# Dummy matmuls and a split weight wait at the start of an attention and GEGLU kernel

## The chip, the cores and the metric

The kernel runs on one NeuronCore of one Trainium2 chip. Its engines are TensorE (PE, the matrix unit; PEld are its weight loads), VectorE (DVE), ScalarE (ACT), GpSimd (POOL) and SyncE (SP). They run side by side and wait for one another on semaphores. SP, ACT and POOL each have a queue on which they issue transfers; the 16 DMA engines of the core serve all of them. The metric is the device time of one execution in microseconds.

## The reference

One sequence of 2048 rows of width 448 goes through a layer norm. The normed rows feed two branches: attention with 16 query heads of width 256 over the last 512 entries of a cache with 8 key and value heads, and a feed-forward network of width 1792. The second branch gates the first.

```python
xn = _layernorm(x)                                  # x: 2048 x 448
q  = xn @ wq                                        # 16 heads x 256
p  = softmax(q @ k[-512:].T * 256**-0.5)            # 8 key heads, each for 2 query heads
s  = (p @ v[-512:]).reshape(2048, 4096) @ wo
g  = silu((gelu(xn @ w_gate) * (xn @ w_up)) @ w_down)
out = x + s * g
```

All inputs and the output are bfloat16.

## The kernel before

The rows are 16 tiles of 128 (t = 0 to 15), and four tiles are one chunk of 512 columns of the transposed activations `xnT`. The width 448 is three blocks of 128 and a rest of 64: `wgu` holds the gate and up weights of the first 384 input rows (k = 0, 1, 2), `wgur` those of the last 64 rows (k = 3, `NK`), gate's on partitions 0 to 63 and up's on 64 to 127.

**Order of the work.** It is written out by hand. Every `K.op` goes to the end of its engine's program; `Plan` finds the waits from the buffers that each operation reads and writes. Operations of PE that write after one another into the same bank do not wait, except where `after` names an operation. An engine runs its program in order, so an operation that waits holds up everything behind it on that engine.

**Stages.** First the head: layer norm of tiles 0 to 3, their transposes by PE and the first feed-forward units of chunk 0. Then the feed-forward units of all four chunks (gate, up, gelu, product), with the down projections between them, then the q projections, scores, softmax, weighted sums and the output projection, chunk by chunk. The layer norm and the transposes of the tiles from 4 on run beside the feed-forward units.

**Loads at the start** (L345 to L352). SP issues x tile 0, the first block of gate weights, x tile 2 and the last rows of gate's first block; ACT issues x tile 1, the first block of up weights, x tile 3 and the last rows of up's first block. Then SP goes on with the other tiles and weight blocks; ACT issues no more.

**The head on PE** (L520 to L552). `warm(20, 3)` issues 20 matmuls on a zeroed buffer into bank 3, whose result nothing reads. `ln_tp_pe(0, ...)` transposes tile 0 in two parts, k = 1, 2 into banks 6 and 7 and k = 0, 3 into banks 4 and 5, and ACT copies each part into `xnT` (L424 to L427). Then `gu_group(HEAD, PH, (0, 1), ((0, 0), (0, 1)))` (L529) starts the units f = 0, 1, 2 on the columns of tile 0 with bank pairs (0, 1), (2, 3) and (4, 5): three passes of part 0 (k = 2, 1), then three of part 1 (k = 0 and the last rows). Each of the six passes has four matmuls of 64 rows and 128 columns. Then come the transposes of tile 1, the second phase of the units on tile 0, the units on tile 1, and so on through tile 3.

**A pass** (`group`, L440 to L463). A unit has a gate bank and an up bank; phase 0 multiplies the upper half of the rows for one and the lower half for the other, and phase 1 the other way round. The last rows (`NK`) belong to phase 0 alone. Each pass waits for all of `reads`, which L473 makes of the unit's weight block, its last rows (`b_wlr`) and a placeholder for the whole weight region. `last_row[b]` remembers the last pass on a bank pair and its phase: a pass of another phase waits for that one on the semaphore of PE.

**DVE's order in the head** is statistics of tiles 0 and 1, scaling of tile 0 and 1, statistics of tile 2, statistics of tile 3, scaling of tile 2, scaling of tile 3. ACT computes the standard deviations and copies the transposes out of PSUM.

Of the kernel before, what the change touches and what calls it, by code (L numbers as in the profile page):

```python
# [11 lines left out]
P = 128  # L12
# [152 lines left out]
def bass_recurrent_scan__sliding_block_cached__geglu_ffn__prompt_kernel(  # L165
# [19 lines left out]
    QC = 512  # L185
# [5 lines left out]
    NK = D // P  # L191
# [6 lines left out]
    HG = 8  # L198
# [3 lines left out]
    with es:  # L202
        K = Plan(nc, es)
        base = [(nc.sbuf_base + 31) // 32 * 32]

        def place(name, shape, dt, at=None):
            size = {BF16: 2, F32: 4}[dt]
            for n in shape[1:]:
                size *= n
            size = (size + 31) // 32 * 32  # L210
            if at is None:
                at = base[0]
                base[0] += size
            assert at + size <= nc.sbuf_usable_end, (name, at + size, nc.sbuf_usable_end)
            return nc.alloc_sbuf_tensor_at(name, list(shape), dt, offset=at), at, at + size

        def sbuf_bufs(at, size, n):
            return [K.buf(at + i * size, size) for i in range(n)]
# [26 lines left out]
        b_xnT = [[K.buf(), K.buf()] for t in range(NT)]  # L245
# [7 lines left out]
        wqr, a, _ = place("wqr", [P, Hq, P], BF16)  # L253
        b_wql = [[K.buf() for i in range(3)] for g in range(NG)]
# [21 lines left out]
        b_wgu = K.buf(a, at - a)  # L276
        FBL = [0, 3, 6, 9, NF]
        b_wl = [[K.buf() for j in range(2)] for i in range(4)]
        b_wlr = [[K.buf() for j in range(2)] for i in range(3)]
# [6 lines left out]
        b_gl = sbuf_bufs(a, QC * 2, NGL)  # L286
# [18 lines left out]
        b_ps = [K.buf() for i in range(8)]  # L305
# [4 lines left out]
        def qs(h):  # L310
            return HG - 1 - h % HG


        def dma(q, o, i, reads=(), writes=()):
            K.op(q, lambda e, o=o, i=i: e.dma_start(o, i), reads, writes, dma=True)  # L315
# [4 lines left out]
        def act(o, i, func, reads, writes, scale=1.0):  # L320
            K.op("act", lambda e, o=o, i=i: e.activation(o, i, func, scale=scale), reads, writes)  # L321

        def mms(lst, reads, writes, after=()):
            def fn(e):
                ins = None
                for (o, l, r, st, sp) in lst:
                    ins = e.matmul(o, lhsT=l, rhs=r, start=st, stop=sp)  # L327
                return ins
            return K.op("pe", fn, reads, writes, after=after)


        def load_x(q, t0, n):
            dma(q, x4[:, t0:t0 + n, :], x_view[:, t0:t0 + n, :], (), b_x4[t0:t0 + n])
# [6 lines left out]
        def load_wr(q, i, j):  # L340
            w = (B_w_gate, B_w_up)[j]
            lo, hi = FBL[i] * P, (FBL[i + 1] if i < 2 else NF) * P
            dma(q, wgur[R * j:R * j + R, lo:hi], w[K3:D, lo:hi], (), (b_wlr[i][j],))
# [3 lines left out]
        load_w("sp", 0, 0)  # L347
        load_w("act", 0, 1)
        load_x("sp", 2, 1)
        load_x("act", 3, 1)  # L350
        load_wr("sp", 0, 0)
        load_wr("act", 0, 1)  # L352
        K.op("pool", lambda e: e.memset(ident[:, :], 0.0), (), (b_ident,))
        K.op("pool", lambda e: e.affine_select(
            out=ident[:, :], in_=ident[:, :], compare_op=ALU.not_equal, fill=1.0, base=0,
# [32 lines left out]
        def ln_recip(t):  # L388
            K.op("dve", lambda e: e.reciprocal(rstd[:, t:t + 1], ve[:, t:t + 1]), (b_ve[t],), (b_rstd[t],))
# [18 lines left out]
        def ln_tp_pe(t, parts):  # L408

            s = t % NXN  # L410
            for i, b in parts:
                tp = pall[b // 2].bitcast(BF16)[:, :].rearrange("p (b k c) -> p k b c", b=2, c=R)
                ks = {None: slice(0, NK + 1), 0: slice(1, 3), 1: slice(0, 4, 3)}[i]

                def fn(e, tp=tp, ks=ks):
                    ins = None
                    for k in range(NK + 1)[ks]:
                        for u in range(2):
                            r = slice(R * u, R * u + R)
                            ins = e.transpose(tp[:, k, u, :], xn[r, s, k * P:(k + 1) * P], ident[r, r])  # L420
                    return ins
                K.op("pe", fn, (b_xn[s][:1] if i == 0 else b_xn[s]) + [b_ident], b_ps[b:b + 2])
            for i, b in parts:
                tp = pall[b // 2].bitcast(BF16)[:, :].rearrange("p (b k c) -> p k b c", b=2, c=R)  # L424
                ks = {None: slice(0, NK + 1), 0: slice(1, 3), 1: slice(0, 4, 3)}[i]
                act(xnT[:, ks, t * P:(t + 1) * P].rearrange("p k (b c) -> p k b c", c=R), tp[:, ks, :, :],
                    ACT.Copy, b_ps[b:b + 2], b_xnT[t] if i is None else b_xnT[t][i:i + 1])  # L427

        def warm(n, b):
            def fn(e):  # L430
                ins = None
                for i in range(n):
                    ins = e.matmul(bank[b][:, 0:256], lhsT=gl[:, 0, 0:P], rhs=gl[:, 0, 0:256], start=True, stop=True)
                return ins
            K.op("pe", fn, (b_gl[0],), (b_ps[b],))


        last_row = {}

        def group(units, lo, hi, start, stop, phases=(0, 1)):  # L440

            for p in phases:
                ph, part = p if isinstance(p, tuple) else (p, None)
                ks = {None: [2, 1, 0, NK], 0: [2, 1], 1: [0, NK]}[part]
                for (b, w, wr, cols, reads, xts) in units:
                    lst = []  # L450
                    for k in ks:
                        if k == NK and ph == 1:
                            continue
                        for u, j in ((0, ph), (1, 1 - ph)):
                            rows = slice(R * u, R * u + R)
                            l = wr[rows] if k == NK else w(j, k)[rows]
                            lst.append((bank[b + j][:, lo:hi], l, xnT[rows, k, cols], start and ph == 0 and k == 2,
                                        stop and ph == 1 and k == 0))
                    before = [last_row[b][0]] if b in last_row and last_row[b][1] != ph else []
                    xb = [y for x in xts for y in (x if part is None else x[part:part + 1])]  # L460
                    o = mms(lst, reads + xb, b_ps[b:b + 2], before)
                    last_row[b] = (o, ph)

        def gu_group(ns, pairs, part=None, phases=(0, 1)):

            lo, hi = (0, QC) if part is None else (part[0] * P, part[1] * P)
            units = []
            for n, b in zip(ns, pairs):
                c, f = divmod(n, NF)
                wi = [j for j in range(4) if FBL[j] <= f][-1]  # L470
                fc = slice(f * P, (f + 1) * P)
                units.append((b, lambda j, k, fc=fc: wgu[:, j, k, fc], wgur[:, fc], slice(c * QC + lo, c * QC + hi),
                              b_wl[wi] + b_wlr[min(wi, 2)] + [b_wgu], b_xnT[c * 4 + lo // P:c * 4 + hi // P]))  # L473
            group(units, lo, hi, lo == 0, hi == QC, phases)

        def bk(pairs, j):
# [21 lines left out]
        def ln_first(t):  # L498
            ln_stats(t)
            ln_std_act(t)  # L500

        def ln_second(t, dup="dve"):
            ln_recip(t)
            ln_norm(t, dup)
# [9 lines left out]
        def ln_b():  # L514
            if ln_t[1] < ln_t[0]:
                ln_norm(ln_t[1])
                ln_tp_dma(ln_t[1])
                ln_t[1] += 1

        warm(20, 3)  # L520
        ln_first(0)
        ln_first(1)
        ln_second(0)
        ln_tp_pe(0, ((0, 6), (1, 4)))
        ln_second(1, "act")
        HEAD, PH = (0, 1, 2), (0, 2, 4)
        T = ((None, 6),)
        ln_first(2)
        gu_group(HEAD, PH, (0, 1), ((0, 0), (0, 1)))  # L529
        ln_tp_pe(1, T)  # L530
        ln_first(3)
# [72 lines left out]
        def q_group(c, h, pairs):  # L604

            units = [(b, lambda j, k, i=i: wq[:, k, (h + i) * Dh + j * P:(h + i) * Dh + (j + 1) * P],
                      wqr[:, h + i, :], slice(c * QC, (c + 1) * QC), b_wql[h // HG], b_xnT[c * 4:c * 4 + 4])
                     for i, b in enumerate(pairs)]
            group(units, 0, QC, True, True)
            for i, b in enumerate(pairs):  # L610
                s = qs(h + i)
                act(qT[:, s, 0, :], bank[b], ACT.Copy, (b_ps[b],), (b_qT[s][0],))
                K.op("dve", lambda v, s=s, b=b: v.tensor_copy(qT[:, s, 1, :], bank[b + 1]),  # L613
                     (b_ps[b + 1],), (b_qT[s][1],))
# [92 lines left out]
        c = NQC - 1  # L707
# [11 lines left out]
        for i in range(2):  # L719
            b = (AB[3], BB[0])[i]  # L720
            lo, hi = ((0, CUT), (CUT, D))[i]
# [57 lines left out]
```

## Time and profile before

| what | value |
|---|---|
| median of 4 runs | 558.36 us (557.53 to 559.59) |
| profiled execution | 559.59 us |
| its span, first to last instruction | 557.8 us |
| PE busy | 549.8 us, 99% of the span |
| DVE, ACT busy | 316.9 us, 274.3 us |
| granted clock of PE | 1.00 |

The span is what the trace covers; about 1.8 us of the profiled execution lie around it. All times in the prediction's rows are microseconds from the start of the span. A row of the time line gives start, duration, engine, line, operation, output and inputs, and in brackets how long the engine had been idle and what ended that. A line can be that of a helper: L327 is every matmul of `mms`, L420 the transposes, L433 the dummy matmuls, L321 ACT's copies and activations, L315 every plain DMA. In rows of DMA issues the last number is the time from issue to landing in us. A table of stretches gives for each stretch its length, the busy time and number of instructions of PE, PEld, DVE, ACT and POOL, the granted clock, the DMA engines' busy share (over 1 where packets overlap) and GB/s.

### The profile page before, as it was taken

To read this page: it belongs to the slowest core of one execution; us is meant where nothing else is said; L and a number is where in the kernel's file an instruction comes from. 1 tells how busy PE (TensorE), PEld (TensorE's weight loads), DVE (VectorE), ACT (ScalarE), POOL (GpSimd) and SP (SyncE) were. 2 spreads that over 40 slices of the span, in tenths; PEclk is the share of its full clock that TensorE was granted. 3 is DMA by queue.
4 is the path that set the end of the run, shared out by engine and by line. 5 is a ranking of instruction groups with operands and counts; after the bars stand their busy time and mean duration, and the time that the engine had idled before them with its cause. 6 is when DMAs were issued, how large, how long until landed. Compare 5 with 4: busy or idle time off the path is not lost.

```text
span 557.8 us, 9780 instructions
## 1 busy us (share of the span) xinstructions
PE 549.8 (99%) x3650; PEld 265.9 (48%) x3650; DVE 316.9 (57%) x816; ACT 274.3 (49%) x728; POOL 32.7 (6%) x64
## 2 busy tenths in 40 slices
PE   7999999999999999999999999999999999999997
PEld 5664444444544444454444445544444454444455
DVE  6683624444377686515848753286685515858722
ACT  4342323444386685504848752085785504758600
POOL 1120750000000000000000000000000000000000
PEclk9999999999999999999999999999999999999999
DMA  9560599501166284312716713166364313807701
GB/s 290 104 163 9 160 292 324 110 1 39 38 114 115 57 152 96 75 35 71 154 37 142 142 25 87 35 139 105 74 153 77 77 34 88 153 20 151 149 11 34
DMA packets 163599, 57.63 MB, mean 103 GB/s; under 512 B 151456, under 2 KB 160672, under 8 KB 163552
## 3 DMA queue, kind: packets, MB, share of 16 engines
q1 hardware_dynamic: 159488, 45.16, 38.9%
q0 software_dynamic: 3296, 11.27, 6.5%
q8 instruction: 29, 0.48, 0.4%
q10 hardware_dynamic: 768, 0.57, 0.3%
q14 instruction: 18, 0.15, 0.1%
HBM read 17.92 MB, written 1.84 MB: 35 GB/s over the span
## 4 chain that ended last, share of the span: by engine, by line
PE 98%; DMA 1%; issue 0%; SPq 0%; ACT 0%; DVE 0%
PE bank L327 98%; DMA wgur<-in_B_w_gate_dram 1%; SPq L315 0%; ACT xnT L321 0%; PE bank L420 0%; DVE tmp L666 0%; DVE ofin L669 0%
## 5 line engine op out<-in xcount | busy, mean ns | idle before, releaser
L627 ACT ACTIVATE p<-bank 128x512 f32<-128x512 f32 x256 | 149.2, 597 | 103.3 <-PE bank L327 102.0
L631 DVE TENSOR_SCALAR pn<-p,rden 128x512 bf16<-128x512 f32 x256 | 124.5, 486 | 16.9 <-DMA pT<-pn 8.0
L327 PE MATMUL bank<-kT,qT 128*128 128x512 bf16 x512 | 121.0, 379 | 0.0
L327 PE MATMUL bank<-pT,va 128*128 128x512 bf16 x512 | 120.8, 379 | 0.0
L327 PE MATMUL bank<-wo,oT 128*128 128x448 bf16 (+2 forms) x544 | 97.7, 341 | 0.0
L327 PE MATMUL bank<-xnT,wq 64*128 64x512 bf16 x768 | 94.7, 376 | 0.0
L327 PE MATMUL bank<-xnT,wgu 64*128 64x512 bf16 (+1 forms) x780 | 84.4, 347 | 3.4 <-DMA wgur<-in_B_w_gate_dram 1.4
L327 PEld LDWEIGHTS bank<-pT,va 128*128 128x128 bf16 x512 | 50.0, 98 | 60.6 <-DMA pT<-pn 0.7
L327 PEld LDWEIGHTS bank<-kT,qT 128*128 128x128 bf16 x512 | 49.5, 98 | 61.6 <-issue 3.4
L327 PEld LDWEIGHTS bank<-wo,oT 128*128 128x128 bf16 x544 | 52.0, 98 | 45.5
L613 DVE CAST qT<-bank 128x512 bf16<-128x512 f32 x64 | 42.9, 692 | 49.3 <-PE bank L327 49.3
L321 ACT ACTIVATE qT<-bank 128x512 bf16<-128x512 f32 x64 | 38.2, 597 | 61.1 <-PE bank L327 59.4
L327 PEld LDWEIGHTS bank<-xnT,wq 64*128 64x128 bf16 x768 | 36.8, 94 | 46.8 <-ACT p L627 1.7
L483 DVE TENSOR_TENSOR actT<-bank,gl 128x512 bf16<-128x512 f32 x56 | 37.8, 690 | 35.5 <-PE bank L327 26.7
L327 PEld LDWEIGHTS bank<-xnT,wgu 64*128 64x128 bf16 x780 | 40.2, 94 | 36.9 <-issue 2.2
L321 ACT ACTIVATE gl<-bank 128x512 bf16<-128x512 f32 x56 | 33.2, 596 | 49.6 <-PE bank L327 46.3
L627 ACT ACTIVATION_READ_ACCUMULATOR p<-bank 128x1 f32 x256 | 52.7, 206 | 0.0
L630 DVE RECIPROCAL rden<-rsum 128x1 f32<-128x1 f32 x256 | 40.4, 158 | 21.5 <-ACT p L627 21.5
L666 DVE SCALAR_TENSOR_TENSOR tmp<-bank,g 128x448 f32<-128x448 f32 (+2 forms) x17 | 10.1, 597 | 72.5 <-PE bank L327 72.5
L650 DVE CAST oT<-bank 128x512 bf16<-128x512 f32 x64 | 43.8, 684 | 6.9 <-PE bank L327 6.9
L327 PE MATMUL bank<-wd,actT 128*128 128x448 bf16 x224 | 43.0, 353 | 0.0
L321 ACT ACTIVATE oT<-bank 128x512 bf16<-128x512 f32 x64 | 39.0, 610 | 7.0 <-PE bank L327 7.0
(38 smaller groups left out, 185.5 us busy)
## 6 DMA issues: line engine op xcount, KB each, us to landing
wo<-in_A_wo_dram POOLq DMA_DIRECT2D x4, 896.0 KB, 18.2
wq<-in_A_wq_dram POOLq DMA_DIRECT2D x2, 1536.0 KB, 9.8
va<-in_A_v_cache_dram POOLq DMA_DIRECT2D x8, 256.0 KB, 13.1
pT<-pn SPq DMA_TRANSPOSE x128, 2.8
xr<-in_A_x_dram POOLq DMA_DIRECT2D x16, 112.0 KB, 2.3
out_dram<-ofin SPq DMA_DIRECT2D x15, 112.0 KB, 1.7
wd<-in_B_w_down_dram SPq DMA_DIRECT2D x1, 1568.0 KB, 7.4
x<-in_A_x_dram SPq DMA_DIRECT2D x2, 448.0 KB, 6.8
```

The costliest lines, as they stand in the source:

```text
L321: K.op("act", lambda e, o=o, i=i: e.activation(o, i, func, scale=scale), reads, writes)
L327: ins = e.matmul(o, lhsT=l, rhs=r, start=st, stop=sp)
L483: K.op("dve", lambda e: e.tensor_tensor(actT[:, c % 2, f, :], bank[b + 1], gl[:, s, :], ALU.mult), (b_ps[b + 1], b_gl[s]), (b_actT[c % 2][ ...
L613: K.op("dve", lambda v, s=s, b=b: v.tensor_copy(qT[:, s, 1, :], bank[b + 1]), (b_ps[b + 1],), (b_qT[s][1],))
L627: K.op("act", lambda e, b=b, r=r, z=z: e.activation(p32[:, z, :], bank[b], ACT.Exp, scale=att_scale, accum_out=rsum[:, r:r + 1]), (b_ps[b] ...
L630: K.op("dve", lambda e, r=r: e.reciprocal(rden[:, r:r + 1], rsum[:, r:r + 1]), (b_rsum[r],), (b_rden[r],))
L631: K.op("dve", lambda e, r=r, z=z, y=y, t=t4 % 2: e.tensor_scalar(pn[:, y, t, :], p32[:, z, :], rden[:, r:r + 1], None, op0=ALU.mult), (b_p ...
L650: K.op("dve", lambda v, i=i, b=b: v.tensor_copy(oT[:, i, :], bank[b]), (b_ps[b],), (b_oT[i],))
L666: K.op("dve", lambda e: e.scalar_tensor_tensor(out=tmp[:, s, c0:c1], in0=bank[b][:, c0:c1], scalar=0.5, in1=g2[:, t, c0:c1], op0=ALU.mult, ...
```

## The change

1. ACT issues the last rows of up's first block ahead of x tile 3. SP's order stays.
2. The last rows of the weights leave `reads` and become `rreads`, which only a pass with `NK` in phase 0 waits for. In the head's split passes that is part 1 alone; a pass that isn't split still waits for both at its first phase. The q projections get the same form.
3. The dummy matmuls at the start go to bank 2 in place of bank 3, claim both banks of the pair, and are entered in `last_row`, so that the next pass on bank pair (2, 3) waits for their end.
4. Three more dummy matmuls follow the transposes of tile 0, before the first passes.

```diff
--- before.py
+++ after.py
@@ -347,9 +347,9 @@
         load_w("sp", 0, 0)
         load_w("act", 0, 1)
         load_x("sp", 2, 1)
-        load_x("act", 3, 1)
         load_wr("sp", 0, 0)
         load_wr("act", 0, 1)
+        load_x("act", 3, 1)
         K.op("pool", lambda e: e.memset(ident[:, :], 0.0), (), (b_ident,))
         K.op("pool", lambda e: e.affine_select(
             out=ident[:, :], in_=ident[:, :], compare_op=ALU.not_equal, fill=1.0, base=0,
@@ -426,16 +426,16 @@
                 act(xnT[:, ks, t * P:(t + 1) * P].rearrange("p k (b c) -> p k b c", c=R), tp[:, ks, :, :],
                     ACT.Copy, b_ps[b:b + 2], b_xnT[t] if i is None else b_xnT[t][i:i + 1])
 
+        last_row = {}
+
         def warm(n, b):
             def fn(e):
                 ins = None
                 for i in range(n):
                     ins = e.matmul(bank[b][:, 0:256], lhsT=gl[:, 0, 0:P], rhs=gl[:, 0, 0:256], start=True, stop=True)
                 return ins
-            K.op("pe", fn, (b_gl[0],), (b_ps[b],))
-
-
-        last_row = {}
+            last_row[b] = (K.op("pe", fn, (b_gl[0],), b_ps[b:b + 2]), None)
+
 
         def group(units, lo, hi, start, stop, phases=(0, 1)):
 
@@ -446,7 +446,7 @@
             for p in phases:
                 ph, part = p if isinstance(p, tuple) else (p, None)
                 ks = {None: [2, 1, 0, NK], 0: [2, 1], 1: [0, NK]}[part]
-                for (b, w, wr, cols, reads, xts) in units:
+                for (b, w, wr, cols, reads, rreads, xts) in units:
                     lst = []
                     for k in ks:
                         if k == NK and ph == 1:
@@ -458,7 +458,8 @@
                                         stop and ph == 1 and k == 0))
                     before = [last_row[b][0]] if b in last_row and last_row[b][1] != ph else []
                     xb = [y for x in xts for y in (x if part is None else x[part:part + 1])]
-                    o = mms(lst, reads + xb, b_ps[b:b + 2], before)
+                    rr = rreads if ph == 0 and NK in ks else []
+                    o = mms(lst, reads + rr + xb, b_ps[b:b + 2], before)
                     last_row[b] = (o, ph)
 
         def gu_group(ns, pairs, part=None, phases=(0, 1)):
@@ -470,7 +471,7 @@
                 wi = [j for j in range(4) if FBL[j] <= f][-1]
                 fc = slice(f * P, (f + 1) * P)
                 units.append((b, lambda j, k, fc=fc: wgu[:, j, k, fc], wgur[:, fc], slice(c * QC + lo, c * QC + hi),
-                              b_wl[wi] + b_wlr[min(wi, 2)] + [b_wgu], b_xnT[c * 4 + lo // P:c * 4 + hi // P]))
+                              b_wl[wi] + [b_wgu], b_wlr[min(wi, 2)], b_xnT[c * 4 + lo // P:c * 4 + hi // P]))
             group(units, lo, hi, lo == 0, hi == QC, phases)
 
         def bk(pairs, j):
@@ -517,11 +518,12 @@
                 ln_tp_dma(ln_t[1])
                 ln_t[1] += 1
 
-        warm(20, 3)
+        warm(20, 2)
         ln_first(0)
         ln_first(1)
         ln_second(0)
         ln_tp_pe(0, ((0, 6), (1, 4)))
+        warm(3, 2)
         ln_second(1, "act")
         HEAD, PH = (0, 1, 2), (0, 2, 4)
         T = ((None, 6),)
@@ -604,7 +606,7 @@
         def q_group(c, h, pairs):
 
             units = [(b, lambda j, k, i=i: wq[:, k, (h + i) * Dh + j * P:(h + i) * Dh + (j + 1) * P],
-                      wqr[:, h + i, :], slice(c * QC, (c + 1) * QC), b_wql[h // HG], b_xnT[c * 4:c * 4 + 4])
+                      wqr[:, h + i, :], slice(c * QC, (c + 1) * QC), b_wql[h // HG][:1], b_wql[h // HG][1:], b_xnT[c * 4:c * 4 + 4])
                      for i, b in enumerate(pairs)]
             group(units, 0, QC, True, True)
             for i, b in enumerate(pairs):
```

## The prediction

> **What bounds the kernel now.** I read the page's engine shares first, then the chain of waits, then the time line of the first 16 us, then the DMA views of the places where the chain leaves TensorE (PE).
>
> ```profile
> PE 549.8 (99%) x3650; PEld 265.9 (48%) x3650; DVE 316.9 (57%) x816; ACT 274.3 (49%) x728; POOL 32.7 (6%) x64
> ...
> PE 98%; DMA 1%; issue 0%; SPq 0%; ACT 0%; DVE 0%
> ```
>
> The second line is the chain's shares: all but 2% of the span is matmul work of PE. The chain in order of time says where the 2% lies:
>
> ```profile
> 2.17 4.76 DMA wgur<-in_B_w_gate_dram
> 6.93 0.38 issue
> 7.31 0.85 PE bank L327 x24
> ...
> 11.39 2.88 PE bank L327 x75
> 14.27 1.32 issue
> 15.59 538.85 PE bank L327 x3431
> ```
>
> From 15.59 to 554.43 us PE runs without a hole that the chain shows. The change adds and removes no real matmul there, so that stretch stays 538.85 us and the tail behind it stays 3.4 us (557.8 - 554.4). Whatever happens must happen before 15.59: the wait for the last weight rows (until 7.31), two small waits for a transposed tile (0.19 us at 8.96, 0.45 us at 10.88), and a hole of 1.32 us at 14.27.
>
> The time line gives the start, step by step:
>
> ```profile
> 1.18 4.19 PE L433 MATMUL bank<-gl 128*128 128x256 bf16 x20 [1.18 <-DVE epst L358]
> ...
> 5.46 0.44 PE L420 MATMUL bank<-ident,xn 64*128 64x64 bf16 x8
> ...
> 5.74 0.66 ACT L321 ACTIVATE xnT<-bank 128x256 bf16<-128x256 bf16 x2 [0.48 <-PE bank L420]
> ...
> 7.14 0.60 DVE L375 BATCH_NORM_STATS2 stats<-x 128x6 f32<-128x448 bf16 x1
> ...
> 7.31 0.57 PE L327 MATMUL bank<-xnT,wgu 64*128 64x128 bf16 x14 [1.41 <-DMA wgur<-in_B_w_gate_dram]
> ...
> 7.98 0.30 PE L420 MATMUL bank<-ident,xn 64*128 64x64 bf16 x8
> ...
> 8.31 0.60 ACT L321 ACTIVATE xnT<-bank 128x512 bf16<-128x512 bf16 x1 [0.75 <-PE bank L420]
> ...
> 8.96 0.34 PE L327 MATMUL bank<-xnT,wgu 64*128 64x128 bf16 x6 [0.19 <-ACT xnT L321]
> ```
>
> The first copies of tile 0 are done at 6.40, yet PE starts the gates at 7.31, for wgur. The DMA issues of 1.6 to 2.4 us, with the time to landing last in the row:
>
> ```profile
> x<-in_A_x_dram SPq DMA_DIRECT2D x1, 112.0 KB, 4.7
> x<-in_A_x_dram ACTq DMA_DIRECT2D x1, 112.0 KB, 5.1
> wgur<-in_B_w_gate_dram SPq DMA_DIRECT2D x1, 48.0 KB, 4.8
> wgur<-in_B_w_up_dram ACTq DMA_DIRECT2D x1, 48.0 KB, 4.9
> ```
>
> x tile 3 (ACT's, issued 1.66) lands at 6.76, gate's rows (SP's, 2.17) at 6.93 to 6.97, up's rows (ACT's, 2.25) at 7.15; PE goes 0.2 us after the last. Now the hole at 14.27: the clock and DMA share over the two idle stretches, and the DMA queues between 13 and 14 us:
>
> ```profile
> 5.90:7.31 1.41, 0.00 (x1) 0.03 (x1) 1.10 (x4) 0.68 (x4) 0.00 (x0) 1.00 1.09 367
> 14.27:15.59 1.32, 0.00 (x0) 0.00 (x1) 1.15 (x2) 0.24 (x1) 0.00 (x0) 1.00 1.19 352
> ```
> ```profile
> q1 hardware_dynamic: 303, 0.37, 100.6%
> q8 instruction: 1, 0.02, 6.3%
> ```
>
> The hole falls inside one pass (5 of its 8 matmuls are before it), where the code has no wait. All DMA engines are full (share over 1). One instruction packet moves just before it, the first of 29 on q8 (0.48 MB). PE's program is 7300 instructions: 0.48 MB over 7300 is 66 bytes each, so q8 fits PE's own program in packets of about 250 instructions, and PE stops after 219 matmuls and as many weight loads. I read the hole as PE out of instructions, their next block stuck behind the weight loads.
>
> **The change part by part.**
>
> *Order of the two DMAs on ACT's queue.* No DMA is added. Up's rows are issued in x tile 3's place (1.66) and x tile 3 at about 2.2; SP's queue is unchanged. SP and ACT have 560 KB each up to here (112+288+112+48) and share the same saturated engines, so the pair's last landing stays near 7.15, and now it is x tile 3's. Up's rows come earlier, by 64 KB of its own queue's bytes at half of 367 GB/s, 0.35 us, at about 6.8; gate's rows stay at 6.93. The last of the two, gate's, so releases PE at 7.13 instead of 7.31: 0.18 us.
>
> *x tile 3 later, 6.76 to about 7.15.* Its statistics start at 7.14 as it is, since DVE is busy until then: cost 0 to 0.1 us on DVE. Behind them on DVE stand the scaling of tile 2 (ends 8.65; PE asks for it at 9.81, or 9.31 after a 0.5 us gain) and of tile 3 (ends 9.93; PE asks at 11.10, or 10.60). Cover 0.66 and 0.67 us: 0 on the path.
>
> *The split wait.* Of the 24 head matmuls, the first 12 (parts k=2,1) no longer wait for wgur. 24 issues took 7.31 to 7.98, 28 ns each, so 12 are 0.34 us taken out from behind the wait. The wait now stands in front of the second 12; queued behind it are those and the transposes of tile 1. Those start at 7.13 + 0.34 = 7.47 instead of 7.98. **Gain at this point 0.5 us.** Bounds: 0.34 if gate's rows slip to up's old landing; 0.84 if both land with tile 3's old slot, 6.4 to 6.5. The later stages that test wgur wait at their first pass as before: 0.
>
> *What is late next.* Transposes to copy to PE (7.98, 8.31, 8.96) is a fixed chain: ACT is free at 7.55, so the copy starts at 7.80 and PE at 8.46. Tile 2's chain (9.81, 10.13, 10.88) and tile 3's follow PE, with the DVE covers above. So 0.5 us reaches 14.27, which becomes 13.77.
>
> *Three dummy matmuls.* By the only row of this shape, 20 in 4.19 us, one costs 0.21 and three 0.63, in 5.90 to 6.53; by the full clock's pace nearer half. The first 12 gates, ready at 6.07 to 6.45, then end at 6.87 at the latest, 0.26 us before wgur releases PE: cost 0. If wgur landed early, up to 0.26 would show. Their benefit: the granted clock is 1.00 through the idle stretch and after it, and the 24 gates run at 28 ns, so there is nothing to win in this execution: 0. The bank number also changes, so the first pass on bank 2 waits for the dummies' end, with a pass on bank 0 before it: 0.
>
> *The hole.* This is the unknown. The block boundary is an instruction number; 6 more instructions put it 3 matmuls (0.1 us) earlier in the program, so 0.1 us more work lies behind the hole. If a block is asked for when the one before is used up, the asking is 125 matmuls before the stop, in the passes of 8.96 to 9.64, at about 9.4; it is asked for 0.5 + 0.1 = 0.6 us earlier. What the hole's end does with that has no row. Bound above: neighbouring loads. The 224 KB of x issued at 7.96 landed 4.7 us later (12.7), the 480 KB of weights issued at 8.59 landed 5.3 later (13.9): in this queue 0.63 us of asking is 1.2 us of landing, so 0.6 earlier may be 1.1 earlier. Bound below: the landing is set by when the loads drain, 0. In between, one for one, 0.6. I take 0.85, between one for one and the neighbours' slope, since those rows are nearest in time, and take off 0.1 for the three matmuls: the long stretch begins at 15.59 - 0.75 = 14.84.
>
> [...] The packet of 13 to 14 us and a stop inside a pass are what the trace has; I go by them.
>
> **The sum.** Profiled execution: 559.59 us, of which the span is 557.8 and 1.8 lies around it. Less 0.75: 558.84. The median of the four runs, 558.36, is 1.23 below the profiled one; the same gain gives **557.6 us**, ratio 0.9987.
>
> **The rivals.**
> 1. *The hole eats the gain.* The block lands when it landed before; PE merely waits longer. Time 558.36 + 0.1 = 558.5. For it: the DMA share is over 1 until 15 us whatever PE does. Against: a request made earlier stands further ahead.
> 2. *The hole closes.* With the block there by 13.77, 0.5 + 1.32 - 0.1 = 1.7 us: 556.6. For it: on the page's later 28 packets no such hole shows. Against: the landing would have to move by 1.9 us for 0.6 of asking.
> 3. *Slower.* The block falls behind one 480 KB weight load more: 1.4 us at 352 GB/s, and 0.1: 559.9; behind two, 561. It decides once the hole ends later than 15.5. For it: loads issued at 8.59 and 9.10 stand right beside the request. Against: the request moves forward, not back.
> 4. *The wait isn't shortened*, because gate's rows land with x tile 3 at 7.15: 0.34 instead of 0.5, 557.8, within the forecast.
>
> **How the numbers follow.** About 0.3% (1.7 us) is what a measurement of this kernel can tell from no change. Forecast with its variants (gain 0.4 to 1.3): 0.45. Hole eats it: 0.15. Hole closes: 0.27. Slower: 0.13. The closing case lies on the bound of 0.3% and with the forecast's upper tail gives faster 0.30; slower 0.12; same 0.58. The range 556.2 to 559.0 holds all but the slower case and the ends: closing reaches 556.6 and a little below, rival 1 reaches 558.5, and the four runs spread by 1 us about their median.
>
> **What would show it.** First 12 gate matmuls before 7 us, a wait for wgur in front of the second 12, transposes of tile 1 at about 7.5, PE's next gates at 8.46. Three L433 matmuls between 5.9 and 6.5. x tile 3's statistics still at about 7.15. The hole near 13.7 with its end near 14.8, the first q8 packet near 12.4. The long stretch still 538.9. Wrong if the long stretch changes, if the tile 2 or tile 3 chain starts to hold PE, or if the hole ends after 15.5 or is gone.

## The result

The changed kernel takes 557.48 us in the median of 43 runs (556.95 to 558.74), the kernel before 558.59 in 67 runs beside it. The ratio is 0.9982, 95% interval 0.9977 to 0.9987: 1.0 us faster, under the 0.3% that the chances went by. Forecast were 557.6 us and a gain of 0.75.

The page of the profile after (span 556.2 us, that execution 558.05) has the same bound, the engine shares and the shares of the chain:

```profile
PE 550.5 (99%) x3653; PEld 260.7 (47%) x3653; DVE 317.1 (57%) x816; ACT 274.2 (49%) x728; POOL 32.7 (6%) x64
...
PE 99%; ACT 0%; issue 0%; DVE 0%
```

The chain in order of time (start, duration, what):

```profile
1.18 4.45 PE bank L435 x20
5.63 0.33 PE bank L420 x5
5.96 0.76 PE bank L435 x3
6.72 0.85 PE bank L327 x18
...
10.81 2.78 PE bank L327 x72
13.59 0.49 issue
14.09 538.78 PE bank L327 x3434
```

The long stretch is as before (538.78 and 538.85 us); it begins at 14.09 instead of 15.59. The DMA wait that stood ahead of the first gates is gone from the chain, and the hole is 0.49 us instead of 1.32. In the time line of the head (L435 is the dummies' line now):

```profile
5.89 0.82 PE L435 MATMUL bank<-gl 128*128 128x256 bf16 x3
...
6.65 0.64 PE L327 MATMUL bank<-xnT,wgu 64*128 64x128 bf16 x14
...
6.79 0.59 DVE L375 BATCH_NORM_STATS2 stats<-x 128x6 f32<-128x448 bf16 x1
...
7.41 0.28 PE L420 MATMUL bank<-ident,xn 64*128 64x64 bf16 x8
...
7.73 0.60 ACT L321 ACTIVATE xnT<-bank 128x512 bf16<-128x512 bf16 x1 [0.53 <-PE bank L420]
...
8.38 0.34 PE L327 MATMUL bank<-xnT,wgu 64*128 64x128 bf16 x6 [0.19 <-ACT xnT L321]
```

The gates start at 6.65 instead of 7.31, the transposes of tile 1 at 7.41 instead of 7.98, and the chain behind them moves along (8.38 instead of 8.96). The statistics of tile 3 (the DVE row) do not wait for their load. The DMA issues of 1.6 to 2.4 us, time to landing last:

```profile
x<-in_A_x_dram SPq DMA_DIRECT2D x1, 112.0 KB, 4.3
x<-in_A_x_dram ACTq DMA_DIRECT2D x1, 112.0 KB, 4.3
wgur<-in_B_w_up_dram ACTq DMA_DIRECT2D x1, 48.0 KB, 4.5
wgur<-in_B_w_gate_dram SPq DMA_DIRECT2D x1, 48.0 KB, 4.2
```

Here is a warning. Gate's rows, whose place in the queue the change leaves alone, landed at 6.4 against 6.9 in the profile of before. The loads of that execution were simply quicker, so the two profiles must not be subtracted: their spans differ by 1.6 us, the medians by 1.1. The packet of the instruction queue that I tied to the hole moves in the window of 11 to 12 us, before in 13 to 14:

```profile
q8 instruction: 1, 0.02, 6.5%
```

Executions of before do not lie evenly. On one chip 22 of 35 took 557.38 to 557.99 us and 13 took 558.55 to 560.36, with nothing between. I call the second the late group and count executions at or over 558.55. On the two other chips of the experiments the executions also fill the space between (6 of 34 and 10 of 35 took 558.00 to 558.54), so there the count is one over a line and not over a gap. The lower the median and the fewer the late executions, the less of the start is lost; the shortest time I take for what the kernel can do when nothing at the start goes late.

| kernel | executions | shortest, us | median, us | late |
|---|---|---|---|---|
| before (all of its runs beside after) | 67 | 557.34 | 558.59 | 34 |
| after | 43 | 556.95 | 557.48 | 2 |

### The profile page after: what moved, and what is told of

Read it like the earlier page. It is cut to its first block, busy times and chain, and to the rows that moved or that the text cites. A ratio compares the mean times of both kernels' runs of the same rounds, so it can differ in the third digit from the quotient of the medians.

```text
span 556.2 us, 9787 instructions
## 1 busy us (share of the span) xinstructions
PE 550.5 (99%) x3653; PEld 260.7 (47%) x3653; DVE 317.1 (57%) x816; ACT 274.2 (49%) x728; POOL 32.7 (6%) x64
## 4 chain that ended last, share of the span: by engine, by line
PE 99%; ACT 0%; issue 0%; DVE 0%
PE bank L327 98%; PE bank L435 1%; ACT xnT L321 0%; PE bank L420 0%; DVE tmp L668 0%; DVE ofin L671 0%; DVE gl L357 0%; DVE epst L358 0%
## 5 line engine op out<-in xcount | busy, mean ns | idle before, releaser
L327 PEld LDWEIGHTS bank<-xnT,wgu 64*128 64x128 bf16 x780 | 35.3, 94 | 39.9 <-issue 1.6
```

## Experiments: one part of the change at a time

These four ran on one chip beside 34 executions of before (shortest 557.42, 19 late; a 35th, of 3337 us, is left out).

**The split wait alone.**

```diff
-                    o = mms(lst, reads + xb, b_ps[b:b + 2], before)
+                    rr = rreads if ph == 0 and NK in ks else []
+                    o = mms(lst, reads + rr + xb, b_ps[b:b + 2], before)
...
-                              b_wl[wi] + b_wlr[min(wi, 2)] + [b_wgu], b_xnT[...]))
+                              b_wl[wi] + [b_wgu], b_wlr[min(wi, 2)], b_xnT[...]))
```

> The kernel before with the split wait alone (order of the loads, dummies and bank as before). The full change measured 0.9982 of before, 1.0 us. Theory A (PE starts earlier, and the block of instructions is asked for earlier, so the hole near 14 us shrinks too): up's rows still land last, the second 12 gates start at about 7.3, the transposes of tile 1 at 7.65 instead of 7.98; 0.3 us there and as much again at the hole: 0.9990, 558.0 us. Theory B (the hole ends when the loads let it, and its size in the two profiles is chance): 1.0000. Theory C (the dummies make the gain, by the clock): 1.0000.

Measured: median 557.71, ratio 0.9988 (0.9973 to 1.0004), shortest 557.33, 3 of 12 late. The chain of its profile:

```profile
2.25 5.39 DMA wgur<-in_B_w_up_dram
7.63 0.14 issue
7.77 0.51 PE bank L327 x12
...
14.39 1.32 issue
15.71 145.38 PE bank L327 x1129
```

The wait does what the code says: it now stands in front of 12 matmuls only. But up's rows came 0.5 us later in this execution, so PE got to the hole as late as in before, and the hole was as long. The interval takes in theory A and no change; the shortest execution moved by 0.09 us.

**The order of the two loads alone.**

```diff
-        load_x("act", 3, 1)
         load_wr("sp", 0, 0)
         load_wr("act", 0, 1)
+        load_x("act", 3, 1)
```

> The kernel before with the order of the two loads on ACT's queue alone. Theory A: gate's rows land last, at 6.95, PE starts the 24 gates at 7.13 instead of 7.31: 0.2 us and as much again at the hole, 0.9994, 558.2 us. Theory B and theory C: 1.0000. If x tile 3's later landing costs anything it shows here as a later copy of tile 3 (after 11.43) or a ratio over 1.0005.

Measured: median 557.25, ratio 0.9972 (0.9957 to 0.9987), shortest 557.04, 1 of 12 late. More than theory A gave it. In its time line the gates wait for gate's rows alone, until 6.47:

```profile
6.47 0.57 PE L327 MATMUL bank<-xnT,wgu 64*128 64x128 bf16 x14 [0.52 <-DMA wgur<-in_B_w_gate_dram]
```

and its chain knows no hole any more:

```profile
10.44 0.12 PE bank L420 x8
10.55 541.39 PE bank L327 x3506
```

**The change without the three dummies.**

```diff
         ln_tp_pe(0, ((0, 6), (1, 4)))
-        warm(3, 2)
```

> The kernel after without the three dummy matmuls behind the first transposes; all else of the change stays. Theory A: the dummies give nothing, and in the profile of after they ended at 6.5 and held the gates until 6.65, so without them PE starts at 6.4 or so: 0.998, 557.4 us, the same as the full change or 0.1 to 0.2 us better. Theory C: without them the gain falls to 0.3 us or less, 0.9995, with matmuls at half pace for some us after 6.4.

Measured: median 557.43, ratio 0.9975 (0.9961 to 0.9989), shortest 556.95, 1 of 12 late. The gain does not rest on the dummies: theory C falls as the explanation of the whole. The shortest is that of the full change.

**The dummies alone** (with bank 2 and the entry in `last_row`).

```diff
-        warm(20, 3)
+        warm(20, 2)
...
         ln_tp_pe(0, ((0, 6), (1, 4)))
+        warm(3, 2)
```

> The kernel before with the dummies alone (the three more, bank 2 in place of 3, the entry in last_row). They lie in the time in which PE waits for wgur until 7.31. Theory A and theory B: 1.0000, at most 6 instructions' worth of an earlier block boundary, within 0.1 us. Theory C: most of the gain is here, 0.9985.

Measured: median 558.08, ratio 0.9987 (0.9974 to 1.0001), shortest 557.37, 4 of 12 late, none over 559.07 (before: up to 561.34). The shortest time stays, as A and B said; whether the lower median is real, 12 executions do not tell. Its profile has the dummies in the gap, and the gates still waiting past them:

```profile
5.89 0.71 PE L435 MATMUL bank<-gl 128*128 128x256 bf16 x3
6.79 0.57 PE L327 MATMUL bank<-xnT,wgu 64*128 64x128 bf16 x14 [0.20 <-ACT xn L321]
```

## Experiments: what the hole is

In all nine profiles with a gap of more than 0.1 us it stands at the same place: ahead of record 449 of PE's own stream, counting matmuls, weight loads and waits from 0. In before and after that is behind 219 matmuls; since after has three dummies more ahead of it, its hole lies three matmuls earlier in the program, inside the same pass. I take a block as 256 records, an estimate from the 255 that lie between two packets on average (7300 matmuls and weight loads over 29 packets give about 250); that puts the asking for it around record 193 (449 less 256). The time at which PE starts record 193 I call "asked"; it is an inference. In the profile of before, from the third packet of the instruction queue to the last, one moves every 255 records of PE on average (176 to 291), which ties the queue to PE's program; but some move up to 41 records before the matching record (193 and every 256th from there). The next four runs move instructions and loads around.

**Fewer instructions ahead** (on after; 10 dummies of 512 columns in place of 20 of 256).

```diff
-        warm(20, 2)
+        warm(10, 2, 512)
```

(`warm` has a third argument here, the number of columns.)

> The kernel after, with the 20 dummy matmuls of 256 columns at the start written as 10 of 512: the same time on PE, 20 instructions less. Theory A (the hole is PE out of its own instructions, at a fixed instruction number, near the 450th recorded one): the stop moves 10 matmuls later in the program, where the matmuls are 512 wide (1.1 us later in time), while the block is asked for only 0.3 us later. The hole shrinks by 0.8 us: none or next to none, 0.2 to 0.4 us better than after, 557.2 us. Theory B (the hole comes at a certain time, from the loads): where a profile has a hole, it starts at 13.4 to 14.3 whatever the program's length, and the time is that of after, 557.5.

Measured: median 557.27, ratio 0.9971 (0.9959 to 0.9982), shortest 556.86, longest 557.69, none late; no hole in the profile (0.04 us at record 449). That is theory A's time; the full change was not run on this chip, and the two intervals against before overlap (full change 0.9977 to 0.9987).

**More instructions ahead** (on after; 80 dummies of 64 columns).

```diff
-        warm(20, 2)
+        warm(80, 2, 64)
```

> The kernel after, with the 20 dummy matmuls at the start written as 80 of 64 columns: the same time on PE, 120 instructions more. Theory A: the stop moves 60 matmuls earlier in the program, to about 11.1 us, and the block is asked for about 2 us earlier; a hole, if there is one, starts at 11 and not at 13.5, and the first instruction packet moves before 10 us. Time 557.0 to 557.8 by how much earlier the block lands. Theory B: first packet and hole as in after (packet at 11.5, hole at 13.6), 557.5.

Measured: median 557.14, ratio 0.9973 (0.9961 to 0.9985), shortest 556.87, longest 557.85, none late. The instruction packet now moves in the window of 8 to 9 us, though the edit moves no load:

```profile
q8 instruction: 1, 0.02, 6.2%
```

So the packet goes by PE's instruction count and not by the loads' time: theory B falls. The stop goes with the count too. A small gap of 0.19 us stands at record 449, now 59 matmuls earlier in the program than in after. It is in the first of these rows; the second is the same six matmuls in after:

```profile
10.37 0.52 PE L327 MATMUL bank<-xnT,wgu 64*128 64x128 bf16 x6
...
10.85 0.35 PE L327 MATMUL bank<-xnT,wgu 64*128 64x128 bf16 x6
```

**The last weight loads held back, on after.**

```diff
-        load_w("sp", 3, 0)
-        load_w("sp", 3, 1)
-        load_x("sp", 8, 4)
...
         gu_group(HEAD[1:], PH[1:], (1, 2), (1,))
+        gate = [last_row[4][0]]
+        for j in range(2):
...
+            K.op("sp", lambda e, o=wgu[:, j, :, lo:hi], i=...: e.dma_start(o, i), (), (b_wl[3][j],), dma=True, after=gate)
+        load_x("sp", 8, 4)
```

> The kernel after, with the last block of weights (two loads of 480 KB) and x tiles 8 to 11 issued on SP only after PE's passes on tile 1, at about 9.7 instead of 8.6 to 9.6. They are needed at 20 us. Theory A with the queue of loads as the reason for the block's delay: the block waits behind less, the first packet moves before 11 us and there is no hole: 0.2 to 0.5 us better than after, 557.1. If only the order of the loads already issued at the time of the asking matters, or if the block is late for another reason, nothing changes: 557.5.

Measured: median 557.61, ratio 0.9977 (0.9964 to 0.9990), shortest 556.93, none late; the packet at 10.25 and no hole in the profile, as theory A had it, but the longest took 558.39. The time is no better than that of after (557.48, not run beside it). The expectation had the time of the held loads wrong: SP's program has two DMA transposes ahead of them, and they went out at 14.0, not 9.7; PE did not wait for them.

**Fewer instructions ahead, on before.**

```diff
-        warm(20, 3)
+        warm(10, 3, 512)
```

> The kernel before, with nothing of the change, and its 20 dummy matmuls written as 10 of 512 columns. Theory A: the hole of before (1.3 us in its profile) shrinks by 0.8 us where there is one, so the slow half of its executions gets faster and the fastest stay: median 0.9988 of before, 558.0. Theory B: 1.0000.

Measured: ratio 0.9991 (0.9976 to 1.0007), 5 of 11 executions late, at 559.20 to 559.66 (a twelfth, of 977 us, is left out). The gap was 0.17 us in its profile, ten matmuls later in the program than in before, at record 449 again; and yet that execution was a late one (559.25). The reason is in the time line: two rows of 24 matmuls of one shape take 1.49 us at 8.53 and 0.85 us at 12.70.

```profile
8.53 1.49 PE L327 MATMUL bank<-xnT,wgu 64*128 64x128 bf16 x24
...
12.70 0.85 PE L327 MATMUL bank<-xnT,wgu 64*128 64x128 bf16 x24
```

PE ran at half pace until about 10.6, and came to record 449 only at 15.9. So the small gap is no test of theory A's 0.8 us. There is a second way to be late, and the profile of before did not show it. That called for the next two.

**The held loads on before** (the edit of the held run above, on the kernel before).

> The kernel before with one edit: the last block of weights (two loads of 480 KB) and x tiles 8 to 11 go out on SP after PE's passes on tile 1 and not at 8.6 to 9.6. In before and in the split-wait run PE's block was asked for at about 9.4 (the time of the 193rd recorded instruction, 256 ahead of the stop), after the second of these loads had gone out at 9.1, its packet moved 3.9 us later and the hole was 1.5; where it was asked for before 9.2 the packet moved 1.8 to 2.8 later and the hole was 0 to 0.7. If the two loads ahead in the queue are the reason: packet within 3 us of the asking, no hole over 0.5, the slow half of before's executions gets 1 us faster, 557.9 us, 0.9988. If the delay has another reason: hole and times as in before, 1.0000.

Measured on a third chip: ratio 0.9993 (0.9983 to 1.0003), median 557.92, 557.43 to 558.40, none of 12 late where before had 13 of 35. The shortest did not move (before: 557.38). The chain still has a hole, but a short one:

```profile
11.04 2.87 PE bank L327 x75
13.92 0.50 issue
14.42 538.85 PE bank L327 x3431
```

With the two loads out of the way (they went out at 14.9) the late group is empty. Were the groups drawn alike, none of the 13 late ones of all 47 would fall among these 12 about once in 95 times. So the held loads (the two, and the x tiles behind them) make late executions when they go out early. What share of the late group is theirs stays open: the median did not move (557.88 for before), and the ratio's interval reaches 1. The profile meets the expectation at its edge (packet 3.04 after the asking, hole of 0.50), but could not show much: its block was asked for at 9.02, no later than in two profiles in which the loads were in place and the hole was 0.16 and 0.04 (table below).

**A late clock on purpose.**

```diff
-        warm(20, 3)
+        warm(20, 3, 16)
```

> The kernel before with its 20 dummy matmuls at the start cut from 256 columns to 16, so that the number of instructions stays and PE is not busy before the transposes. In the run of before with 10 wide dummies the matmuls kept half pace until 10.6 us and the executions fell in two groups, 557.4 to 558.0 and 559.2 to 559.7. Theory C2 (the slow group of before is executions in which the clock opens late, because PE is idle from 5.9 to 7.3): here the clock opens late in every execution, first gates at half pace, and all times are in the slow group or above it, 559.3 to 561. If the slow group is the hole alone, or the loads: the times stay spread as in before, 558.5.

Measured beside the same executions of before: median 559.25, ratio 1.0020 (1.0009 to 1.0031), all 12 late, 558.97 to 560.16. Its profile has no hole (0.04 us at record 449), and the half pace lasts until 11.2:

```profile
1.18 0.70 PE L433 MATMUL bank<-gl 128*128 128x16 bf16 x20 [1.18 <-DVE epst L358]
...
8.01 1.49 PE L327 MATMUL bank<-xnT,wgu 64*128 64x128 bf16 x24
...
12.56 0.86 PE L327 MATMUL bank<-xnT,wgu 64*128 64x128 bf16 x24
```

A late clock alone puts an execution into the late group. How many of before's late executions it makes stays open: one profile of before's kind (10 dummies) showed it, and the held run, with none late of 12, leaves it at most one execution in five or so (0.78 to the 12th is 5%), where 13 of 35 were late.

**After, and after with more instructions, on the same chip.**

> The kernel after itself, on the chip of these runs, to be set beside the next one and beside the two groups of before: no execution over 558.7, median 557.5.

> The kernel after with 80 dummy matmuls of 64 columns at the start, again, now beside after on one chip. Theory A (earlier asking removes what is left of the hole, 0.7 us in the profile of after): 0.2 to 0.4 us better than after in the median, 557.1 to 557.3, and the fastest executions the same. Theory B: the same as after.

Measured: after 557.65, ratio 0.9987 (0.9977 to 0.9998), 557.15 to 558.13; with 80 dummies of 64 columns 557.24, ratio 0.9982 (0.9974 to 0.9991), 556.81 to 557.55. In the medians 0.4 us apart; the longest of the second is shorter than the median of the first. Its chain has no hole:

```profile
10.58 0.12 PE bank L420 x8
10.70 541.50 PE bank L327 x3506
```

So this version beats both kernels, by 0.4 us over after. The expectation had the fastest executions stay; they moved as well (557.15 to 556.81). In both profiles PE starts the matmul in front of after's stop at 13.27; after then loses 0.2 us at record 449. The rest of the 0.3 us between these two executions is lost later. That the earlier asking makes the whole 0.4 us is not shown.

The profiles side by side, times in us:

| profile | first gate | asked | first packet | packet after asking | loads moved by then, KB | record 449 after packet | gap at record 449 |
|---|---|---|---|---|---|---|---|
| before, fewer | 7.07 | 10.68 | 13.63 | 2.95 | 3923 | 2.42 | 0.17 |
| late clock | 6.55 | 9.70 | 12.30 | 2.60 | 3517 | 2.65 | 0.04 |
| split wait alone | 6.78 | 9.49 | 13.35 | 3.87 | 3724 | 2.35 | 1.54 |
| before | 7.31 | 9.37 | 13.22 | 3.85 | 3673 | 2.37 | 1.54 |
| no dummies | 6.61 | 9.16 | 11.54 | 2.38 | 3093 | 2.47 | 0.16 |
| fewer, on after | 6.63 | 9.11 | 11.40 | 2.29 | 3071 | 2.62 | 0.04 |
| before, loads held | 6.96 | 9.02 | 12.06 | 3.04 | 3073 | 2.36 | 0.71 |
| dummies alone | 6.79 | 8.74 | 11.09 | 2.35 | 3042 | 2.51 | 0.16 |
| after | 6.65 | 8.67 | 11.51 | 2.83 | 3079 | 2.58 | 0.71 |
| after again | 6.61 | 8.57 | 10.90 | 2.33 | 2970 | 2.59 | 0.21 |
| order alone | 6.47 | 8.53 | 10.35 | 1.83 | 2805 | 2.86 | 0.04 |
| after, loads held | 6.29 | 8.25 | 10.25 | 2.00 | 2809 | 2.70 | 0.02 |
| more, beside after | 6.60 | 6.67 | 8.00 | 1.33 | 1979 | 2.86 | 0.00 |
| more | 6.23 | 6.30 | 8.11 | 1.81 | 2015 | 2.57 | 0.19 |

(The gap is from the start of the last matmul in front of record 449 to the start of that record; the chain counts 0.22 us less. Loads moved are all packets of the two load queues that started before the first instruction packet.)

Two things stand in this table. First, the packet ends the hole: wherever there is a gap over 0.1 us, PE goes on 2.35 to 2.59 us after the packet starts to move, and in the five profiles without one PE comes to record 449 later than that, 2.62 to 2.86 us after it. Second, the packet comes behind the loads. What was issued up to 7.96 us is 3072 KB, and the next two loads are the 480 KB ones of 8.6 and 9.1. In eight profiles 2805 to 3093 KB had moved before the packet; in the four that were asked for after 9.3 it was 3517 to 3923 KB, so that one or both of the big loads had gone ahead, in part at least. With the loads held on before, the packet moved only when everything issued ahead had moved, and the DMA engines had run nearly empty (share 0.25 from 11.5 to 12.0). The time from asking to packet alone is no such measure: it is 3.9 us at 9.4 and 9.5, but 2.6 and 2.9 in the two runs at half pace, whose asking is the least certain.

## Why the prediction was right, and where it was not

- **Everything happens before the long stretch.** Right in these two profiles: 538.85 and 538.78 us.
- **A gain of 0.5 us ahead of the hole.** As far as is known the sum was right and its division wrong. By the shortest executions beside the same before, order and split together give 0.47 us (557.42 to 556.95), the order alone 0.38, the split alone 0.09. I had 0.18 and 0.34. The shortest of 12 is a coarse measure, but the medians rank the two alike (557.25 and 557.71). In the order's profile PE started 0.09 us after the rows had landed, where I had kept the 0.2 of before. That accounts for 0.1 us; where the rest of the order's share comes from is not shown.
- **x tile 3 later costs nothing.** Right: DVE took up its statistics at 6.79, directly behind those of tile 2.
- **The dummies cost nothing.** Right: with and without them the shortest execution was 556.95, and the medians were 557.48 and 557.43. Where the clock was still low (its record in the trace of after begins at 6.85) they did what the bound said and a little more: the gates started at 6.65, after them, instead of 6.53 at the latest.
- **The dummies win nothing.** This step is the one that failed in its reasoning. I read the granted clock of 1.00 in the idle stretch and closed the case. That was one execution: the clock record of its trace begins at 4.97 us, and the rows print 1.00 ahead of that too, although the first dummies follow one another every 0.213 us until then and 0.110 us after it. With the three dummies the record began at 4.5 to 7.2 in all seven profiles; without them at 4.7 to 5.9 in five, and at 10.59 in one, which was late (the run made late on purpose not counted). My estimate from these times is that filling the gap could help only executions whose clock would start in between. That it does so in the full change is not shown: 2 of 43 late with them, 1 of 12 without.
- **The hole is PE out of instructions.** Right: it stands at record 449 with 10 matmuls less and with 60 more ahead, its packet moves with the instruction count, and it ends 2.35 to 2.59 us after that packet.
- **The end of the hole.** I took 0.85 us earlier for an asking 0.6 earlier, between one for one and the neighbouring loads' slope. In the two profiles the asking moved by 0.70 and the packet by 1.71: steeper than any row I used. The predicted hole of 1.1 us was 0.49, and none to speak of in the runs of the order, of the dummies and of the second run of after. This is the term that was mis-sized, and with it the gain, 1.0 for 0.75. I had looked for a slope; the table shows a step: asked for 0.7 us earlier, the packet moved behind 3079 KB of loads instead of 3673, so that the load of 8.6 us no longer went ahead of it. That the forecast of 557.6 lies within 0.2 us of the median is in part luck: the four runs that it starts from had a median 0.23 below that of the 67.
- **The rivals.** "The hole eats the gain" and "slower" are ruled out by the interval. "The hole closes" all but happened in the profile of after's second run (a gap of 0.21 us, nothing in the chain) but not of its first (0.71); its 556.6 us is below every execution of after. "The wait isn't shortened" did not: in the order's profile gate's rows landed at 6.4 and x tile 3 at 6.6.
- **The packets behind the first.** As rival 2 has it, the chain of before shows no hole behind the other 28 packets. The first moved with the DMA engines full (100.6% for the loads' queue between 13 and 14 us of before).

## What to carry to other kernels

A hole inside a group of matmuls that wait for nothing may be the engine's own instructions: look whether an instruction packet moves just before it (here 2.35 to 2.59 us ahead of the hole's end) and whether it stays at the same instruction when code is added ahead (here record 449). While the queues fill with loads, being half a microsecond earlier can be worth a whole one, where the request then stands in front of the next big load (here, asked for 0.70 us earlier, the packet moved 1.71 us earlier, with 3079 KB ahead of it in after and 3673 in before). Of the parts tried alone here, the order of two small transfers, moved at no cost, gave the most. And where executions of a kernel fall into groups, one profile shows one of them: set the shortest, the median and the share of late ones beside each other before a wait or a clock is called harmless.

## What was not expected of the hardware

- **The clock's start.** In the traces the stretches at full clock last 546.13, 549.55 or 552.96 us, 3.41 to 3.42 apart. They do not begin at one time: at 4.97 in before, at 6.85 in after, at 4.5 to 7.2 in the seven profiles with the three dummies. A late start cost 1.5 us here (559.25 against the early group of about 557.7).
- **Waits far from the change.** In three profiles (split wait alone, no dummies, dummies alone) PE also waited twice for transposed probabilities between 160 and 381 us, with gaps of 0.4 to 0.6 us between matmuls, and the long stretch was longer by that. Single gaps of 0.3 to 0.4 us stand there in before and in after's second run too, so they belong to no one part of the change.
- **The same load, half a microsecond apart.** Gate's rows, issued at about 2.2 in every kernel, landed between 6.1 and 7.5 us. That spread is as large as the gain that was looked for.
- **An issue beside the packet.** In the two profiles of after with 80 dummies, SP's issue of x at 7.96 took 1.50 and 1.35 us instead of 0.59, and the 480 KB loads went out 0.75 to 0.9 us later, though the edit leaves the loads alone. The first instruction packet moved at 8.11 and 8.00; what held the issue was not tested.
